# First loads through another queue and a re-planned order: attention and channel mix on one core

## The chip, the cores and the metric

The kernel runs on one core of a Trainium2 chip. A core has TensorE (matrix products, into the accumulation memory PSUM), VectorE, ScalarE and GpSimd (elementwise work), and SyncE, which issues DMAs; GpSimd issues DMAs too. Each engine runs its own instructions in a fixed order, and waits on semaphores for the others. The metric is the device time of one execution in microseconds. Seven runs of the kernel before took 241.66 to 243.84 us, with a median of 242.81.

## The reference

Two stages, with 8 batches, 8 heads, 576 positions, head size 64, in fp32:

```python
rel = pos[:, None] - pos[None, :]
mask = (rel >= 0) & (rel < 128)
scores = where(mask, q @ k.T / sqrt(64) - slopes[h] * abs(rel), -1e9)
x = (softmax(scores) @ v) with heads side by side      # [8, 576, 512]

x_prev = x shifted by one position
xk = mu_k * x + (1 - mu_k) * x_prev
xr = mu_r * x + (1 - mu_r) * x_prev
kk = relu(xk @ w_k) ** 2                               # 512 -> 1024
out = sigmoid(xr @ w_r) * (kk @ w_v)                   # 1024 -> 512
```

## The kernel before

All products run in bf16. A batch is worked in four groups of two heads. A window of 128 positions over tiles of 128 means that a key tile meets only its own query tile and the next one, so scores are computed key by query in strips (line 548), exponentiated by ScalarE (line 559), and multiplied with v on TensorE (line 603); a column of ones beside v gives the row sums, whose reciprocal (line 609) scales the result (line 614). The bias comes in one of two ways. For the first `NBIAS` groups TensorE adds it before the exponential (line 535, from the distances `dist` and a scaled identity `sid`); later VectorE multiplies the exponentials with a table (line 572). The result is turned by TensorE (line 641), copied by ScalarE to `xt` (line 518, as all of `copy_any`), and VectorE makes the difference to the shifted copy (line 667) and the two mixtures `xk` and `xr` (line 674).

The channel mix takes stretches of 256, 384 or 512 positions: eight times four products with w_k (line 754), a relu on ScalarE (761), a square on VectorE or ScalarE (727, 725; `SQ` says who may), then for each tile of 128 positions four products with w_r (772), a tanh on ScalarE (779), eight products with w_v (786), and one VectorE operation that joins both (797) and is stored by SyncE (803).

Queries and keys must lie with the head dimension on the partitions. Batches 1 to 3 are loaded and turned by TensorE (line 918, then a ScalarE copy of 128x1024). Batches from 4 on (`XB`) are turned by DMA transposes that SyncE issues (`flip`, line 397). Batch 0 is worked in two parts, positions 0 to 255 and the rest, so that work can start early: its part 0 of groups 0 and 1 comes in fp32 through SyncE (`first_load`, line 409) into `stage`, is cast to bf16 on ScalarE or VectorE and turned on TensorE (line 850). Part 0 of groups 2 and 3, and part 1 of all, come through GpSimd's queue, whose DMAs cast on their way (`half_load`, line 368).

All other loads stand in GpSimd's queue, in the order of the string `LOADS`: `v` and `V` the first and second half of v of batch 0, `0` and `1` queries and keys of part 0 for groups 2 and 3, `K` and `k` the halves of w_k, `2` and `3` queries and keys of part 1, `t` the last 64 positions, `a`, `b`, `c` batch 1, `R` w_r, `W` and `w` the halves of w_v. The batches 2 to 7 follow.

The order of the instructions on the engines is not written by hand. The kernel adds each piece of work to a `Plan` with an estimated duration, what it depends on, and a priority; `Plan.run` fills the engines in estimated time, and the order that comes out is what the program holds. `A`, `SLOPE`, `NBIAS`, the estimates in `dma` and `flip`, and the lists of engines that may do a thing are inputs to this plan: change one and many instructions move. `NWARM` = 90 products on a tile of zeros (line 509) keep TensorE running at the beginning, with the lowest priority.

Constant columns, those of ones beside v, the pads of `at`, `xt`, `tt` and the unused half of `tv`, are set by VectorE memsets in the opening (line 336).

Of the kernel before, what the change touches and what calls it, by code (L numbers as in the profile page):

```python
# [150 lines left out]
def kernel(  # L151
# [27 lines left out]
    RELU_SCALE = 0.5 ** 0.5  # L179

    NQ, NA, NX, NV, NC = 4, 4, 3, 2, 2
    XB = range(4, B)
    XO = range(6, B)
    X0 = 16
    NWARM = 90
    LOADS = 'v01Kk23tVabcRWw'
    XD = 4
    OTL = 5.0
    NO = 4

# [3 lines left out]
    def SQ(order):  # L194
        return (DVE, ACT) if order < 10 else (DVE,)

    def XT(b, g):
        return (ACT,)

# [3 lines left out]
    def many(n, shape, dtype, name):  # L203
# [10 lines left out]
        "p (a i r h d) -> p a i r h d", a=2, i=2, r=2, d=D)  # L214
    stage = qx_buf[1].rearrange("p i g s -> p (i g s)").bitcast(FP32)[:, 0:8 * 2 * D].rearrange(
        "p (i g h w) -> p i g h w", i=2, g=2, h=2)
    at_buf = many(NA, [128, 2 * 1024 + 64], BF16, "at")
# [29 lines left out]
    def one(h):  # L247
        return uno[h.idx if h.cls == "p1" else N1 + h.idx]

    def two(h):  # L250
# [4 lines left out]
                {})  # L255
    PE, ACT, DVE, POOL, SPE, FAB, VIR = "PE", "ACT", "DVE", "POOL", "SP", "FAB", "VIR"
    LAT = {PE: 0.2, ACT: 0.22, DVE: 0.16}

    def mm(n):
        return max(n / 2400.0 + 0.0025, 0.029)  # L260
# [7 lines left out]
    AHEAD = 30.0  # L268
    A = {PE: 9.00, ACT: 7.00, DVE: 5.50, VIR: 0}
    NBIAS = 4  # L270
    XRL = 3.0
    MODE = 0
    EARLY = 0.0
    SLOPE = 4.8

# [22 lines left out]

    def dma(queue, kb, issue, emit, deps=(), need=(), free=(), after=()):
        n = plan.add(queue, issue, 0.0, list(deps) + [last.get(queue)],  # L300
                     (len(plan.nodes),), emit, need)
        last[queue] = n
        return plan.add(FAB, kb / 290.0, 0.9, [(n, 1.0)], (len(plan.nodes),),
                        None, (), free)
# [30 lines left out]
    def memset(t, v, dur=0.08, late=0):  # L335
        return dve_op(dur, lambda e: nc.vector.memset(t, v), [], (0, 20 + late))
# [6 lines left out]
    n_ident = dve_op(0.11, emit_ident, [n_iota], (0, -1))  # L343
    blank, blank_t, blank_v = [], [], []
    for t in range(NA):
        blank.append(memset(at_buf[t][:, 2048:2112], 1.0))
        blank.append(memset(at_buf[t][:, 1024:1088], 1.0))
    for t in range(NV):
        blank_v.append(memset(vs_buf[t][:, :, :, D], 1.0, 0.08, -21))
    for t in range(2):  # L350
        blank.append(memset(xt_buf[t][:, :, X0 - 2:X0], 0.0))
        blank.append(memset(tt_buf[t][:, :, 1], 0.0))
    for t in range(NV):
        blank_t.append(memset(tv_buf[t][64:128], 0.0, 0.5, 1))
        blank_t.append(memset(tv_buf[t][0:64, :, D], 1.0, 0.08, 1))

    def issue_t(nd):
# [36 lines left out]
    def flip(b, i, j, g):  # L396
        return dma(SPE, 290, 1.3, lambda e: nc.sync.dma_start_transpose(
            out=qx_buf[xbh[b].idx][:, i, :, 128 * j:128 * j + 128],
            in_=cb_buf[ch[b].idx][:, i, j].rearrange("p h d -> p (h d)")),
            [g, (cl[b][NF * i + j], 6.0)], (), [ch[b]])  # L400
# [4 lines left out]

    def first_load(i, g):
        hs = (q, k)[i][0, 2 * g:2 * g + 2]
        dst = stage[:, i, g]
        return dma(SPE, 128, 0.46, lambda e: nc.sync.dma_start(
            out=dst, in_=hs[:, 0:256].rearrange("h (p r) d -> p h (r d)", p=128)))  # L410

    def mu_load(i, src):
        return dma(SPE, 4, 0.5, lambda e: nc.sync.dma_start(
            out=mu_row[NPO * i:NPO * i + NPO], in_=src.rearrange("(po p) -> po p", p=128)))
# [4 lines left out]
    src0 = {}  # L419
    for g in range(2):  # L420
        for i in range(2):
            src0[i, g] = [first_load(i, g)]
    n_row = [mu_load(0, moe_mu_k), mu_load(1, moe_mu_r)]
# [3 lines left out]
    def load_step(what):  # L427
        if what in "01":
            for r in range(2):
                rs_ = half_load(int(what), 0, r, 4, 8)  # L430
                for g in (2, 3):
                    src0.setdefault((int(what), g), []).append(rs_)
        elif what in "vV":
            for j in ((0, 1) if what == "v" else (2, 3)):
                vl[0].append(v_load(0, j, vh[0], [gv[0]] + blank_v))
                if j == 0:
                    n_w["d"] = pool_op(0.55, emit_cut, [n_ident, last[POOL]])
                    last[POOL] = n_w["d"]
            if what == "V":
                vl[0].append(tv_load(0, vh[0]))  # L440
        elif what in "23":
            src1.extend(half_load(int(what) - 2, 1, r, 0, 8) for r in range(2))
        elif what == "t":
            th[0], tl[0] = tail_load(0)
        elif what in "Kk":
            j = int(what == "k")
            n_w["k", j] = w_load(wk_sb[:, :, 512 * j:512 * j + 512],
                                 moe_w_k[:, 512 * j:512 * j + 512], 780)
        elif what == "R":
            n_w["r"] = w_load(wr_sb, moe_w_r, 840)  # L450
        elif what in "Ww":
            j = int(what == "w")
            n_w["v", j] = w_load(wv_sb[:, 4 * j:4 * j + 4], moe_w_v[512 * j:512 * j + 512], 790)
        elif what in "abc":
            batch_load(1, what)
# [41 lines left out]
    def emit_mu(e):  # L497
# [3 lines left out]
        out=id_row, in_=ident[0:2 * NPO, 0:2 * NPO]), [n_ident], (0, 3))  # L501
    n_mut = plan.add(PE, 0.1, LAT[PE], n_row + [n_idr], (0, 0), emit_mu, [h_mu])
    n_muk = n_mur = plan.add(DVE, 0.08, LAT[DVE], [n_mut], (0, 4), lambda e: nc.vector.tensor_copy(
# [8 lines left out]
    for i in range(NWARM):  # L512
        plan.add(PE, 0.1 if i < 40 else 0.056, 0.0, [n_warm, g_wm], (1e12, i), emit_warm, (), [h_wm])

# [224 lines left out]
    def channel_mix(P, c0, c1, first, xks, xrs, order):  # L739
# [27 lines left out]
        for i, c in enumerate(range(c0 // 128, c1 // 128)):  # L767
# [13 lines left out]
            hv, ho = Hold("p1"), Hold("ot")  # L781
            o = 128 * c - c0

            def emit2(e, half, hv=hv, o=o):
                for fo in range(4 * half, 4 * half + 4):
                    nc.tensor.matmul(  # L786
                        one(hv), lhsT=kk_buf[hk.idx][:, fo, o:o + 128], rhs=wv_sb[:, fo],
                        start=(fo == 0), stop=(fo == NFO - 1))
            m0 = op(PE, NPO * mm(512), squares[0:4] + [n_wv[0]], place(),
                    lambda e, f=emit2: f(e, 0), [hv], [hk])  # L790
            m1 = op(PE, NPO * mm(512), squares[4:8] + [n_wv[1], m0], place(),
                    lambda e, f=emit2: f(e, 1), (), [hk])

            pe_mix.extend((m0, m1))

            def emit_o(e, hv=hv, hs=hs, ho=ho):
                nc.vector.scalar_tensor_tensor(  # L797
                    out=ot_buf[ho.idx], in0=rs_buf[hs.idx], scalar=1.0, in1=one(hv),
                    op0=ALU.add, op1=ALU.mult)
            d = op(DVE, dve_t(512), [m1, t], place(), emit_o, [ho], [hv, hs])  # L800
            row = SP * P + 128 * c
            y = plan.add(SPE, 0.6, 0.0, [d], (1, len(plan.nodes)),
                         lambda e, ho=ho, row=row: nc.sync.dma_start(
                out=of[row:row + 128, :], in_=ot_buf[ho.idx]))
            plan.add(FAB, 0.8, 0.9, [(y, 1.0)], (0,))
            plan.add(VIR, 0.0001, 0.0, [(y, OTL)], (0,), None, (), [ho])

# [22 lines left out]
    for part in range(2):  # L830
        if part == 1:
            htt, n_tt = tails(0, (0, 0, 1, 0))
        for g in range(G):
            prio = (0, 0, part, g)
            if part == 0 and g < 2:
                cs = []
                for i in range(2):
                    cs.append(op((ACT, DVE), {ACT: act_t(256, True), DVE: dve_t(256, 2)},
                                 src0[i, g], prio + (0,), lambda e, i=i, g=g: copy_any(
                        e, half_buf[:, 0, i, :, 2 * g:2 * g + 2].rearrange("p r h d -> p h r d"),  # L840
                        stage[:, i, g].rearrange("p h (r d) -> p h r d", d=D))))
            else:
                cs = src0[0, g] + src0[1, g] if part == 0 else src1
            hp = Hold("p1")

            def emit_t(e, part=part, g=g, hp=hp):
                for i in range(2):
# [7 lines left out]
                   [hp] + ([hq0[g]] if part == 0 else []))  # L855
            y = op((ACT, DVE), {ACT: act_t(512), DVE: dve_t(512)}, [t], prio + (3,),
                   lambda e, part=part, g=g, hp=hp: copy_any(
# [6 lines left out]
            for j, (pieces, m0) in enumerate(PART[part]):  # L864
# [7 lines left out]
            t0, t1 = ((0, 2), (2, NJ))[part]  # L872
            r, hx = attend(0, g, t0, t1, ha, es + vl[0][0:2] + (vl[0][2:] + blank_t if part else []) + blank,
                           prio)
# [107 lines left out]
```

## Time and profile before

| | us |
|---|---|
| median of 7 runs | 242.81 |
| profiled execution, whole | 241.43 |
| its span, first to last instruction | 239.7 |
| TensorE busy | 226.1 (94%), 2183 products |
| VectorE busy | 185.6 (77%) |
| ScalarE busy | 164.4 (69%) |
| GpSimd busy | 105.1 (44%) |
| first product of the channel mix (L754) | starts at 16.48 |
| first product with w_r (L772) | starts at 40.00 |
| last product (L786) | ends at 235.7 |

The profile takes one execution apart. Busy time alone says little of what a change is worth; the chain that ended last is followed back from the last instruction, at each step to what released it, and shows which engine or DMA set the end in which part of the span. A group in the profile is named by its line, engine, what it writes and what it reads, with buffer numbers left out. Products on TensorE overlap, so that one listed with 379 ns starts 0.215 us after the one before it. The clock that TensorE was granted is 1.00 nearly everywhere, with 0.50 for 3.41 us after 16.19.

### The profile page before, as it was taken

The page shows a single profiled execution, that of the slowest core. Times are in us where ns is not written, and L with a number is a line of the kernel's source. Part 1 is how long each engine was busy: PE and PEld are TensorE (multiplying, and loading weights), DVE is VectorE, ACT ScalarE, POOL GpSimd, SP SyncE. Part 2 cuts the span into 40 slices and gives each one's busy share as a digit, 9 for nine tenths or more (in the row PEclk, how much of TensorE's full clock was granted, in tenths as well). Part 3 has the DMA queues.
Part 4 walks back from the last instruction along what each step waited for, and adds up shares of the span by engine and source line. Part 5 has one row for each costly group of instructions (what it writes and reads, how often), then busy time and mean ns, then how long its engine had stood idle before and what let it go on. Part 6 is the DMA issues. An engine that isn't in the chain of part 4 may idle for free.

```text
span 239.7 us, 5684 instructions
## 1 busy us (share of the span) xinstructions
PE 226.1 (94%) x2183; PEld 139.1 (58%) x2211; DVE 185.6 (77%) x407; ACT 164.4 (69%) x289; POOL 105.1 (44%) x132
## 2 busy tenths in 40 slices
PE   8979977999999999799999999999999999999993
PEld 8647564666666765355655666455655754445561
DVE  7575596799998989579897989985789975894342
ACT  3468989779997986778496895957482925326260
POOL 8958995598998961069405953300000000000000
PEclk9988999999999999999999999999999999999998
DMA  8999999999999999999998999996331214221212
GB/s 122 129 178 139 147 130 186 169 180 190 195 139 172 169 165 130 204 164 159 165 195 74 158 163 158 200 134 155 90 100 54 80 54 91 88 88 46 88 45 88
DMA packets 141755, 32.23 MB, mean 134 GB/s; under 512 B 133528, under 2 KB 137120, under 8 KB 141728
## 3 DMA queue, kind: packets, MB, share of 16 engines
q0 software_dynamic: 113104, 16.52, 112.0%
q1 hardware_dynamic: 28624, 15.35, 31.7%
q8 instruction: 17, 0.28, 0.5%
q14 instruction: 10, 0.08, 0.1%
HBM read 33.56 MB, written 9.44 MB: 179 GB/s over the span
## 4 chain that ended last, share of the span: by engine, by line
PE 75%; DMA 14%; POOL 5%; ACT 2%; issue 2%; DVE 1%; POOLq 0%; DVEq 0%
PE uno L786 25%; PE uno L754 22%; PE uno L772 12%; PE duo L603 6%; PE duo L548 5%; DMA wk_sb<-in_moe_w_k_dram 4%; DMA qx<-cb 4%; DMA wr_sb<-in_moe_w_r_dram 3%; DMA vs<-in_v_dram 3%; PE uno L641 2%; POOL vs L371 2%; POOL qx L368 1%; PE uno L918 1%; ACT at L559 1%; POOL cb L393 1%
## 5 line engine op out<-in xcount | busy, mean ns | idle before, releaser
L754 PE MATMUL uno<-xk,wk_sb 128*128 128x256 bf16 (+2 forms) x413 | 71.7, 318 | 1.5 <-ACT xt L518 0.7
L559 ACT ACTIVATE at<-duo 128x1024 bf16<-128x1024 f32 (+2 forms) x68 | 65.1, 1001 | 10.3 <-PE duo L548 10.2
L786 PE MATMUL uno<-wv_sb,kk 128*128 128x512 bf16 x274 | 69.8, 379 | 0.8 <-issue 0.2
L761 ACT ACTIVATE rl<-uno 128x256 bf16<-128x256 f32 (+2 forms) x104 | 47.0, 493 | 22.9 <-PE uno L754 22.3
L754 PEld LDWEIGHTS <-wk_sb 128*128 128x128 bf16 x416 | 39.5, 99 | 25.0 <-issue 2.6
L371 POOL DMA_DIRECT2D vs<-in_v_dram x32 | 28.4, 903 | 30.8 <-PE duo L603 27.0
L786 PEld LDWEIGHTS <-kk 128*128 128x128 bf16 x288 | 26.1, 98 | 26.1
L572 DVE TENSOR_TENSOR at<-at,mask 128x1024 bf16<-128x1024 bf16 x56 | 37.2, 681 | 4.9 <-ACT at L559 4.7
L727 DVE TENSOR_TENSOR kk<-rl 128x256 bf16<-128x256 bf16 (+2 forms) x77 | 25.6, 342 | 17.9 <-ACT rl L761 16.5
L779 ACT ACTIVATE rs<-uno 128x512 bf16<-128x512 f32 x36 | 22.2, 617 | 24.9 <-PE uno L772 24.8
L772 PE MATMUL uno<-wr_sb,xr 128*128 128x512 bf16 x133 | 35.9, 379 | 2.0 <-DMA wr_sb<-in_moe_w_r_dram 1.5
L797 DVE SCALAR_TENSOR_TENSOR ot<-rs,uno 128x512 f32<-128x512 bf16 x36 | 24.5, 683 | 13.6 <-PE uno L786 8.5
L393 POOL DMA_DIRECT2D cb<-in_k_dram x28 | 24.8, 893 | 9.2 <-DMA wv_sb<-in_moe_w_v_dram 3.3
L674 DVE SCALAR_TENSOR_TENSOR xk<-dl,mu_sb,xt 128x576 bf16<-128x576 bf16 (+2 forms) x36 | 26.4, 746 | 0.5
L674 DVE SCALAR_TENSOR_TENSOR xr<-dl,mu_sb,xt 128x576 bf16<-128x576 bf16 (+2 forms) x36 | 26.3, 740 | 0.0
L393 POOL DMA_DIRECT2D cb<-in_q_dram x28 | 24.9, 910 | 2.2 <-DMA vs<-in_v_dram 0.7
L603 PEld LDWEIGHTS <-at 128*128 128x128 bf16 x576 | 21.9, 98 | 5.8 <-ACT at L559 0.3
L772 PEld LDWEIGHTS <-xr 128*128 128x128 bf16 x144 | 13.5, 98 | 15.7 <-DMA wr_sb<-in_moe_w_r_dram 1.7
L518 ACT COPY xt<-uno 128x576 bf16<-128x576 bf16 (+2 forms) x28 | 15.9, 578 | 7.6 <-PE uno L641 7.6
L603 PE MATMUL duo<-vs,at 128*128 128x65 bf16 x448 | 19.1, 194 | 0.1
L614 DVE TENSOR_TENSOR xu<-duo,rc 128x640 bf16<-128x640 f32 x20 | 16.4, 820 | 0.5
L667 DVE TENSOR_TENSOR dl<-xt 128x576 bf16<-128x576 bf16 (+2 forms) x36 | 14.7, 421 | 2.3 <-ACT xt L518 2.0
(64 smaller groups left out, 219.1 us busy)
## 6 DMA issues: line engine op xcount, KB each, us to landing
out_dram<-ot SPq DMA_DIRECT2D x36, 256.0 KB, 3.6
vs<-in_v_dram POOLq DMA_DIRECT2D x32, 128.0 KB, 6.5
cb<-in_q_dram POOLq DMA_DIRECT2D x28, 128.0 KB, 7.5
cb<-in_k_dram POOLq DMA_DIRECT2D x28, 128.0 KB, 8.9
wk_sb<-in_moe_w_k_dram POOLq DMA_DIRECT2D x2, 512.0 KB, 7.6
wv_sb<-in_moe_w_v_dram POOLq DMA_DIRECT2D x2, 512.0 KB, 10.8
ts<-in_q_dram POOLq DMA_DIRECT2D x8, 64.0 KB, 7.7
ts<-in_k_dram POOLq DMA_DIRECT2D x8, 64.0 KB, 7.6
```

The lines of the kernel that those rows point to most:

```text
L371: return dma(POOL, 256, issue_t(1024), lambda e: nc.gpsimd.dma_start(out=vs_buf[h.idx][:, j, :, 0:D], in_=v[b, :, 128 * j:128 * j + 128].r ...
L393: return [dma(POOL, 256, issue_t(1024), lambda e, r=r: nc.gpsimd.dma_start(out=cb_buf[h.idx][:, i, r], in_=src[:, :, r]), [g]) for r in ra ...
L559: lambda e, ah=ah, w=w, hp=hp: nc.scalar.activation(out=ah(), in_=two(hp)[:, :, 0:w], func=AF.Exp, scale=float(scale)), (), [hp])
L572: nc.vector.tensor_tensor(out=a, in0=a, in1=m, op=ALU.mult)
L603: nc.tensor.matmul(a[:, hl, t - t0], lhsT=at[:, lo:lo + 128], rhs=vs[:, u, 2 * g + hl, :] if u < NF else tvb[:, 2 * g + hl], start=(u == u ...
L674: lambda e: nc.vector.scalar_tensor_tensor(out=buf[hk.idx][:, g, e0 + c0:e0 + c1], in0=dls(), scalar=mu[:, g:g + 1], in1=xc(1), op0=ALU.mu ...
L727: nc.vector.tensor_tensor(out=out, in0=in_, in1=in_, op=ALU.mult)
L754: nc.tensor.matmul(one(hp)[:, 0:n], lhsT=wk_sb[:, po, 128 * fo:128 * fo + 128], rhs=xk_buf[hx.idx][:, po, c0:c1], start=(po == 0), stop=(p ...
L761: a = op(ACT, act_t(n), [s], pr, lambda e, hp=hp, hr=hr: nc.scalar.activation(out=rl_buf[hr.idx][:, 0:n], in_=one(hp)[:, 0:n], func=AF.Rel ...
L772: nc.tensor.matmul(one(hp), lhsT=xr_buf[hx.idx][:, po, 128 * c:128 * c + 128], rhs=wr_sb[:, po], start=(po == 0), stop=(po == NPO - 1))
L786: nc.tensor.matmul(one(hv), lhsT=kk_buf[hk.idx][:, fo, o:o + 128], rhs=wv_sb[:, fo], start=(fo == 0), stop=(fo == NFO - 1))
L797: nc.vector.scalar_tensor_tensor(out=ot_buf[ho.idx], in0=rs_buf[hs.idx], scalar=1.0, in1=one(hv), op0=ALU.add, op1=ALU.mult)
```

## The change

Batch 0's part 0 now comes whole through SyncE: after the four loads of groups 0 and 1 two larger ones bring groups 2 and 3, into a `stage` of twice the size. All eight casts are ScalarE's, the copies after the transposes may be ScalarE's or VectorE's. The loads `0` and `1` leave GpSimd's queue; `K` moves up behind the first half of v, and `k` moves back behind the second half of v. The memsets of the pads are split: those of v's column of ones, of the middle pads of `at` and of `xt` stay at the front, the others (`blanks`) are put behind the fourth SyncE load in the plan. The last tile of the output is computed in two column pieces, 384 and 128 wide, each with its own products, join and store. Batch 4 leaves `XB`, so TensorE turns it as it does batches 1 to 3. ScalarE may take squares in the first 3 stretches of the channel mix, and no more in the first 10. `NBIAS` goes from 4 to 5, and the plan's inputs `A`, `SLOPE`, the DMA rate and latency, the estimate of a flip and of a few short operations are changed.

The diff, cut to its core:

```diff
-    XB = range(4, B)
+    XB = range(5, B)
-    LOADS = 'v01Kk23tVabcRWw'
+    LOADS = 'vK23tVkabcRWw'
+    FIN = 384
+    RATE = 284.0
+    FLIP = 1.25
     def SQ(order):
-        return (DVE, ACT) if order < 10 else (DVE,)
+        return (DVE, ACT) if order < 3 else (DVE,)
+    XT0 = (ACT,)
+    QK0 = (ACT, DVE)
+    CAST = (ACT,)
-    stage = qx_buf[1].rearrange("p i g s -> p (i g s)").bitcast(FP32)[:, 0:8 * 2 * D].rearrange(
-        "p (i g h w) -> p i g h w", i=2, g=2, h=2)
+    stage = qx_buf[1].rearrange("p i g s -> p (i g s)").bitcast(FP32).rearrange(
+        "p (i g h w) -> p i g h w", i=2, g=4, h=2)
-    A = {PE: 9.00, ACT: 7.00, DVE: 5.50, VIR: 0}
-    NBIAS = 4
+    A = {PE: 8.75, ACT: 4.50, DVE: 6.75, VIR: 0}
+    NBIAS = 5
-    SLOPE = 4.8
+    SLOPE = 4.7
-        return plan.add(FAB, kb / 290.0, 0.9, [(n, 1.0)], (len(plan.nodes),),
+        return plan.add(FAB, kb / RATE, lat[1], [(n, lat[0])], (len(plan.nodes),),
                         None, (), free)
...
+    blank_v = [memset(vs_buf[t][:, :, :, D], 1.0, 0.09, -21) for t in range(NV)]
     for t in range(NA):
-        blank.append(memset(at_buf[t][:, 2048:2112], 1.0))
-        blank.append(memset(at_buf[t][:, 1024:1088], 1.0))
+        memset(at_buf[t][:, 1024:1088], 1.0)
     for t in range(2):
-        blank.append(memset(xt_buf[t][:, :, X0 - 2:X0], 0.0))
-        blank.append(memset(tt_buf[t][:, :, 1], 0.0))
-    for t in range(NV):
-        blank_t.append(memset(tv_buf[t][64:128], 0.0, 0.5, 1))
-        blank_t.append(memset(tv_buf[t][0:64, :, D], 1.0, 0.08, 1))
+        memset(xt_buf[t][:, :, X0 - 2:X0], 0.0)
+    def blanks(after):
...
+        for t in range(2):
+            late(tv_buf[t][64:128], 0.0, 0.55)
+            late(tv_buf[t][0:64, :, D], 1.0)
+        for t in range(2):
+            late(tt_buf[t][:, :, 1], 0.0, 0.17)
+        for t in range(NA):
+            late(at_buf[t][:, 2048:2112], 1.0)
...
-    def first_load(i, g):
-        hs = (q, k)[i][0, 2 * g:2 * g + 2]
-        dst = stage[:, i, g]
+    def first_load(i, g, n):
+        hs = (q, k)[i][0, 2 * g:2 * g + 2 * n]
+        dst = stage[:, i, g:g + n].rearrange("p g h w -> p (g h) w")
...
-    for g in range(2):
+    for g, n in ((0, 1), (1, 1), (2, 2)):
         for i in range(2):
-            src0[i, g] = [first_load(i, g)]
+            x = first_load(i, g, n)
+            for j in range(g, g + n):
+                src0[i, j] = [x]
+    blank = blanks(src0[1, 1][0])
     def load_step(what):
-        if what in "01":
-            for r in range(2):
-                rs_ = half_load(int(what), 0, r, 4, 8)
-                for g in (2, 3):
-                    src0.setdefault((int(what), g), []).append(rs_)
...
-                vl[0].append(tv_load(0, vh[0]))
+                vl[0].append(tv_load(0, vh[0], blank[0:4]))
...
+            final = row + 128 == B * S
...
+            for a, b in ((0, FIN), (FIN, 512)) if final else ((0, 512),):
+                for half in range(2):
+                    first = a == 0 and half == 0
+                    m = op(PE, NPO * mm(b - a), squares[4 * half:4 * half + 4] +
+                           [n_wv[half], m], place(),
+                           lambda e, f=emit2, h=half, a=a, b=b: f(e, 4 * h, 4 * h + 4, a, b),
+                           [hv] if first else [], [hk])
+                    pe_mix.append(m)
+                d = op(DVE, dve_t(b - a), [m, t], place(),
+                       lambda e, f=emit_o, a=a, b=b: f(e, a, b), [ho] if a == 0 else [], [hv, hs])
...
-            if part == 0 and g < 2:
+            if part == 0:
...
-                    cs.append(op((ACT, DVE), {ACT: act_t(256, True), DVE: dve_t(256, 2)},
+                    cs.append(op(CAST, {ACT: act_t(256, True), DVE: dve_t(256, 2) + 0.08},
...
-            y = op((ACT, DVE), {ACT: act_t(512), DVE: dve_t(512)}, [t], prio + (3,),
+            y = op(QK0, {ACT: act_t(512), DVE: dve_t(512)}, [t], prio + (3,),
...
-            r, hx = attend(0, g, t0, t1, ha, es + vl[0][0:2] + (vl[0][2:] + blank_t if part else []) + blank,
+            r, hx = attend(0, g, t0, t1, ha, es + vl[0][0:2] + (vl[0][2:] + blank if part else []),
                            prio)
```

## The prediction, made before the result was known

> **What bounds the kernel now.** I read the chain that ended last, whole and then in order of time, next TensorE's waits, then busy time by stage. Engine shares of the chain first:
>
> ```profile
> PE 75%; DMA 14%; POOL 5%; ACT 2%; issue 2%; DVE 1%; POOLq 0%; DVEq 0%
> ```
>
> The same chain over the first 45 us (start us, us, what):
>
> ```profile
> 3.81 3.02 POOL qx L368 x4
> 6.83 0.72 POOL wk_sb L403
> 7.54 8.51 DMA wk_sb<-in_moe_w_k_dram
> ...
> 31.79 8.16 DMA wr_sb<-in_moe_w_r_dram
> 39.95 0.05 issue
> 40.00 0.39 PE uno L772
> ```
>
> Until 40 us the chain is GpSimd's load queue; from then on it is TensorE without a break but one. The first is four loads of query and key heads standing in the queue ahead of the weights. The waits of TensorE say how much is lost after the opening:
>
> ```profile
> PE uno L772 <- DMA wr_sb<-in_moe_w_r_dram: 1.5, 1, 1.5
> PE duo L548 <- DMA qx<-cb: 1.3, 1, 1.3
> ```
>
> The second is batch 4 waiting for its last transposing DMA at 97.8. Busy time by stage (stage and length, TensorE, its weight loads, VectorE, ScalarE, GpSimd; clock, DMA share, GB/s):
>
> ```profile
> 0.00:16.48 16.48, 13.39 (x164) 10.64 (x165) 10.79 (x53) 7.15 (x13) 13.37 (x23) 0.99 1.26 142
> 16.48:40.00 23.52, 20.10 (x249) 14.06 (x248) 16.52 (x46) 21.05 (x45) 20.62 (x25) 0.93 2.35 146
> 40.00:97.00 57.00, 56.38 (x639) 37.16 (x648) 52.13 (x100) 49.31 (x82) 41.73 (x50) 1.00 2.21 169
> 97.00:100.00 3.00, 1.67 (x16) 0.69 (x16) 2.02 (x4) 2.36 (x5) 0.00 (x0) 1.00 1.73 203
> 100.00:235.76 135.76, 134.55 (x1120) 76.55 (x1136) 103.51 (x206) 84.56 (x147) 29.33 (x35) 1.00 1.02 116
> ```
>
> TensorE is 99% busy from 40 on, so the span splits in three: the moment T at which the first multiplication by w_r starts (39.95), TensorE's work behind it (235.68 - 39.95 = 195.7, of which 1.5 is the gap at 97.8), and the tail (239.7 - 235.7 = 4.0):
>
> ```profile
> 233.08 2.60 PE uno L786 x12
> 235.68 0.04 DVEq L797
> 235.72 0.04 issue
> 235.76 0.69 DVE ot L797
> ```
>
> One store follows: 3.25 us from the end of that VectorE row to the end of the span. The change touches all three parts.
>
> **Work behind T.** The listing of instructions shows what moves.
> - Batch 4 takes its queries and keys by 32 TensorE transposes instead of eight transposing DMAs. The chain shows eight such transposes of L918 in 0.45 us: +1.8 us. Four copies of 128x1024 come to ScalarE (1057 ns each in the L518 row, +4.2 us); in 40-97 it is busy 49.3 of 57, and it gives squares away, so I put them at nothing. Without that cover they would cost at most 4.2.
> - The gap of 1.5 us at 97.8 goes. Late next would be batch 5's transposing DMAs. Before, they were issued behind batch 4's and landed by 107, while in the new order 80 us of TensorE's work stand between T and the first product that needs them, which puts it near 118. Eight issues of 1.2 to 2.2 us leave SyncE's queue; what stands beside batch 5's eight is one output store behind the first. So no new gap: -1.5.
> - Eight w_k multiplications (256 wide; 28 take 3.06 us in the chain, 0.11 each) move ahead of T: -0.87 here, paid in the opening.
> - 17 of ScalarE's 27 squares (rows of L725) become VectorE's. By the rows of L727 VectorE gains 9 x 0.288 + 3 x 0.355 + 5 x 0.420 = 5.8 us, and loses two mask products of 0.681, because batch 1's first group takes its bias on TensorE. VectorE is 91% busy in 40-97. In the listing, counting row durations, VectorE's work from batch 1's first to batch 6's first reciprocal goes from 143 - 29 = 114 to 144 - 27 = 117 us, and TensorE's for the same stretch from 115 to 113. That is tight, but VectorE overlaps neighbours, so its own time is less than the sum. Between 0 and 4.4 us; I take 0, since the VectorE work listed ahead of batch 1's first reciprocal falls from 29.4 to 27.1 us, a head start of 2.3.
> Sum: 195.7 - 1.5 + 1.8 - 0.9 = **195.1**.
>
> **Tail.** The last tile's eight w_v products become eight of 384 columns, then eight of 128. Columns and so TensorE's time stay the same. VectorE's last operation shrinks from 0.69 (512) to near the 0.42 of the 256-wide product of L614, or less: -0.3 to -0.4. The last store carries 64 KB instead of 256; the transfer's gain I bound between 0 (the first piece's 192 KB go ahead of it, and SyncE issued stores in 0.33 to 0.54 us each) and -0.9 (192 KB less at the 203 GB/s of the row 97-100). I take -0.15, near the first bound, as both pieces must pass one queue within half a us. In all -0.5: **3.5**.
>
> **The opening, T.** Two conditions, the later one counts.
>
> *w_r landed.* Removed from GpSimd's queue: the 3.02 us of issue above. w_k's first half, which landed at 13.5 (6.81 + 6.7), is then issued near 3.8. The second half goes behind the second-half queries and keys, two tails and the rest of v. The bytes do not vanish: two SyncE loads of 256 KB share the DMA engines. Here a rule speaks against the change. The Trainium skill (DMA: Bandwidth & Descriptors, "Issuing engines are not separate DMA queues") says that DMAs from SyncE and GpSimd interleave on the same 16 engines, so a second issuer saves only issue time; and its "Rules for kernel authors" give a load that casts to GpSimd. By the rule w_r gains 1 us (3.0 less about 2 for the moved bytes). By the row more: DMA moved 116 GB/s in 0-9.4 and 178 in 9.4-16.3, so it was short of issued work in the first stretch, and in the second the first w_k half was late although nothing else was queued. I take 2.5, between 1.0 and 3.0: landing at 37.5.
>
> *TensorE reaches it.* ScalarE paces 16-40: 21.05 of 23.52, against 7.15 of 16.48 earlier. All eight fp32 casts (405 ns; two were ScalarE's) now stand in its order, five before the first exponential and three before the second, so that one waits for the last SyncE load. SyncE's small loads landed 2.4 to 3.6 us after issue; the last two are issued near 2.8 and 3.3, carry twice the bytes and share the engines, so I take 7.5 and 8.8. First exponential then at 7.5 (before 7.48), second at 10 (9.48), third 12.2 (12.60), fourth 13.6 (13.3), the last copy of part 0 at 16.3 (16.05). The casts use time in which ScalarE sat idle (3.18 us before 7.48); without that cover they cost 6 x 0.405 = 2.4. The gain comes after: second-half queries and keys, landed at 20 before, are there before 16, so part 1's transposes start at about 15.9 instead of 20.27. From 16.3 on, ScalarE's listed work until batch 1's copies, counted from each start to the next since neighbours overlap, is 3 copies (0.50), 8 masks (0.33), 4 + 4 exponentials (0.70, 0.50), 8 relus (0.30), 3 squares (0.32) and 4 copies (0.35): 13.7 us, ready at 30.0 against 31.36. Batch 1's loads, which landed at 31.0, come 2.5 earlier too. Then 7.1 us as before to TensorE's idle at 38.5, plus what moved ahead: 0.87 and four bias products (0.215 each in L772's row of the chain), 0.86, of which some 0.7 falls into the 1.6 us of small gaps there: 30.0 + 7.1 + 1.0 = **38.1**.
>
> So T = 38.1, set by ScalarE and TensorE and no more by w_r. w_r's stall is gone, ScalarE is late next.
>
> A second rule is weighed. The granted clock was 0.50 from 16.19 to 19.60:
>
> ```profile
> 16.19:19.60 3.41, 3.08 (x14) 0.50 2.42 156
> ```
>
> That row cost 1.7 us of TensorE. The Trainium skill (TensorE: Matmul & The Clock Gate, "Part 4: PE-mode transpose") says that transposes do not count as activity, and Part 1 that full speed needs a busy window of about 3.4 us. TensorE now resumes with 20 transposes where 20 matmuls stood: by the rule the half clock lasts a window longer, +1.7. By the row the part is paced by ScalarE, so neither is worth much; I take 0, and keep both ends, -1.7 and +1.7.
>
> **Sum.** 38.1 + 195.1 + 3.5 = 236.7 against 239.7: -3.0. The profiled execution took 241.43, so 238.4; the median of the runs shown is 1.4 above it (242.81). Measured times are medians, so I forecast 242.81 - 3.0 = **239.8**, own range 238.4 to 241.3.
>
> **Rivals.**
> 1. *The queue delivers at once.* w_r at 37.0, half clock gone, ScalarE gains the 1.7: T near 36.6. 36.6 + 195.1 + 3.5 = 235.2, so 238.3. For it: queue issue led the chain. Against: ScalarE 90% busy in 16-40.
> 2. *The opening gains nothing.* The last SyncE loads turn with v and w_k packet by packet and land as late as GpSimd's did (10.5; TensorE waited for them until 10.59). Both later exponentials shift by 2 us and T is 40.3; what is left is -1.5 + 1.8 - 0.9 - 0.5, some -0.8: 242.0. This is also the case that the change doesn't do what it says.
> 3. *VectorE becomes the bound* (slower). Place: 40 to 150, where it takes the squares. Price: the 4.4 us above, if none of its idle 4.9 us in 40-97 can be used, because each idle piece is a wait for ScalarE; TensorE then waits for VectorE's products before the next multiplication. 236.7 + 4.4 = 241.1, so 244.3. It decides once over two thirds of the added work goes uncovered. For it: 91%; against: the head start.
>
> **Chances.** Forecast 0.52, rival 1 0.18, rival 2 0.16, rival 3 0.14. No change means within 0.5%, 241.6 to 244.0, about what the runs' spread of 241.66 to 243.84 lets one tell. Faster: nearly all of the forecast, rival 1 and a quarter of rival 2, 0.71; same 0.16; slower 0.13. The range runs from rival 1 less the half clock's rest, 237.6, to the far side of rival 2, 243.2.
>
> **What will show it.** Right: first w_r multiplication near 38 without a DMA wait; part 1's transposes before 17; no wait of L559 for a transposing DMA; ScalarE over 90% busy from 16 to 38; end of span less than 3.6 after TensorE's last product. Wrong: w_k's second half or v late and TensorE waiting for it near 22; a second exponential after 11; VectorE named in TensorE's waits between 40 and 150; a half clock beyond 20.

## The result, and the profile after

| | before | after |
|---|---|---|
| median, us (runs, lowest to highest) | 242.56 (31, 241.09 to 244.86) | 238.99 (12, 238.33 to 240.65) |
| ratio, 95% interval | | 0.9852, 0.9825 to 0.988 |
| profiled execution / its span, us | 241.43 / 239.7 | 239.1 / 237.3 |
| first w_r product starts (T) | 40.00 | 38.41 |
| from T to the end of the last product | 195.67 | 196.05 |
| from there to the end of the span | 4.0 | 2.8 |

The kernel is 3.57 us faster: 238.99, where 239.8 was forecast with a range of 237.6 to 243.2. The profiled spans differ by less, 2.4 us, for the profile of the kernel before was taken in one of its quicker executions: 241.43, 1.1 under the median, where that of the kernel after (239.1) lies at its median.

In the page after, the chain that ended last has these shares by engine:

```profile
PE 84%; ACT 6%; DMA 4%; POOL 2%; issue 2%; DVE 0%; POOLq 0%; DVEq 0%; ACTq 0%
```

DMA had 14% of it. The chain over the first 45 us in order of time (start us, us, what) shows what is gone:

```profile
4.60 2.59 POOL qx L381 x3
7.19 9.53 DMA qx<-in_k_dram
17.04 1.08 ACT qk L529 x2
...
30.41 1.05 PE uno L935 x16
...
34.94 2.00 ACT at L570 x2
...
38.84 0.59 PE uno L783 x2
```

The load of w_r, 8.16 us of this chain before, is no longer in it; T is reached through ScalarE's exponentials and relus and TensorE. What is left of the DMAs is the second half of the keys, which landed at 16.72 (20.0 before). Busy time by stage (stage and length, TensorE, its weight loads, VectorE, ScalarE, GpSimd; clock, DMA share, GB/s):

```profile
0.00:15.60 15.60, 12.33 (x164) 9.62 (x165) 10.31 (x49) 8.70 (x17) 12.34 (x21) 1.00 1.48 167
15.60:38.41 22.81, 20.31 (x262) 14.48 (x262) 15.62 (x45) 21.10 (x47) 19.99 (x24) 1.00 2.07 160
38.41:97.00 58.59, 57.69 (x653) 37.83 (x661) 52.83 (x103) 50.88 (x81) 40.86 (x50) 1.00 2.10 169
97.00:100.00 3.00, 3.00 (x35) 1.77 (x34) 3.00 (x8) 3.00 (x6) 0.00 (x0) 1.00 1.09 111
```

Three things are to be seen. ScalarE is busy 21.10 of the 22.81 us ahead of T, 93%: it sets the pace there. TensorE is busy for the whole of 97 to 100, where it stood 1.3 us before, for batch 4 needs no transposing DMA now. And the granted clock is 1.00 in every row shown, with no 3.41 us at half speed.

TensorE's waits (line, what it waited for: us in total, times, longest) hold no DMA wait for w_r or for `qx<-cb`, but behind T a new one:

```profile
PE uno L799 <- DVE ot L804: 0.7, 1, 0.7
```

It lies in the tail, as the end of the chain shows:

```profile
230.99 2.18 PE uno L799 x12
...
233.24 0.56 DVE ot L804
233.81 0.04 issue
233.85 0.62 PE uno L799 x8
234.47 0.02 issue
234.50 0.29 DVE ot L804
```

The products of the second column piece start only when VectorE has read the first: the start of the second group comes 0.87 us later than the usual distance between products. The diff suggests why: both pieces use one `hv`, so one PSUM buffer, and the read of one part of it holds up the writes to the other. An experiment below tests it.

### The profile page after: what moved, and what is told of

It reads as the page before. It is cut to its first block, busy times and chain, and to the rows that moved or that the text cites. A ratio compares the mean times of both kernels' runs of the same rounds, so it can differ in the third digit from the quotient of the medians.

```text
span 237.3 us, 5756 instructions
## 1 busy us (share of the span) xinstructions
PE 225.9 (95%) x2225; PEld 140.0 (59%) x2255; DVE 186.8 (79%) x420; ACT 164.9 (69%) x283; POOL 102.6 (43%) x128
## 4 chain that ended last, share of the span: by engine, by line
PE 84%; ACT 6%; DMA 4%; POOL 2%; issue 2%; DVE 0%; POOLq 0%; DVEq 0%; ACTq 0%
PE uno L799 26%; PE uno L765 25%; PE uno L783 13%; PE duo L614 7%; PE duo L559 6%; DMA qx<-in_k_dram 4%; PE uno L935 3%; PE uno L652 2%; ACT qk L529 2%; ACT at L570 1%; ACT rl L772 1%; POOL qx L381 1%; ACT xt L529 1%; PE uno L716 1%; ACT mask L900 1%
## 5 line engine op out<-in xcount | busy, mean ns | idle before, releaser
L799 PE MATMUL uno<-wv_sb,kk 128*128 128x512 bf16 (+2 forms) x282 | 69.8, 373 | 1.7 <-DVE ot L804 0.7
L765 PE MATMUL uno<-xk,wk_sb 128*128 128x256 bf16 (+2 forms) x412 | 69.2, 313 | 0.4 <-ACT rl L772 0.2
L772 ACT ACTIVATE rl<-uno 128x256 bf16<-128x256 f32 (+2 forms) x104 | 47.9, 486 | 16.5 <-PE uno L765 14.8
L765 PEld LDWEIGHTS <-wk_sb 128*128 128x128 bf16 x416 | 38.9, 98 | 21.7 <-issue 0.2
L738 DVE TENSOR_TENSOR kk<-rl 128x256 bf16<-128x256 bf16 (+2 forms) x94 | 30.4, 338 | 15.5 <-ACT rl L772 14.4
L799 PEld LDWEIGHTS <-kk 128*128 128x128 bf16 x296 | 26.6, 98 | 26.4 <-issue 0.9
L583 DVE TENSOR_TENSOR at<-at,mask 128x1024 bf16<-128x1024 bf16 x54 | 36.1, 677 | 4.0 <-ACT at L570 4.0
L783 PE MATMUL uno<-wr_sb,xr 128*128 128x512 bf16 x133 | 36.4, 379 | 0.6
L804 DVE SCALAR_TENSOR_TENSOR ot<-rs,uno 128x512 f32<-128x512 bf16 (+2 forms) x37 | 24.6, 666 | 14.1 <-PE uno L799 10.5
L529 ACT COPY qk<-uno 128x1024 bf16<-128x1024 bf16 (+1 forms) x20 | 18.1, 943 | 4.3 <-PE uno L935 2.7
```

What stands on the lines that cost most here:

```text
L529: (nc.scalar.copy if e == ACT else nc.vector.tensor_copy)(out=out, in_=in_)
L583: nc.vector.tensor_tensor(out=a, in0=a, in1=m, op=ALU.mult)
L738: nc.vector.tensor_tensor(out=out, in0=in_, in1=in_, op=ALU.mult)
L765: nc.tensor.matmul(one(hp)[:, 0:n], lhsT=wk_sb[:, po, 128 * fo:128 * fo + 128], rhs=xk_buf[hx.idx][:, po, c0:c1], start=(po == 0), stop=(p ...
L772: a = op(ACT, act_t(n), [s], pr, lambda e, hp=hp, hr=hr: nc.scalar.activation(out=rl_buf[hr.idx][:, 0:n], in_=one(hp)[:, 0:n], func=AF.Rel ...
L783: nc.tensor.matmul(one(hp), lhsT=xr_buf[hx.idx][:, po, 128 * c:128 * c + 128], rhs=wr_sb[:, po], start=(po == 0), stop=(po == NPO - 1))
```

## The experiments

Kernels that start from the one after are "after with ..."; the others start from the one before. T and the work behind it are from each one's profiled execution. The kernel before was run again beside each set of experiments, with medians of 241.94, 242.52 and 241.69 us, where it had 242.56 beside the kernel after; so differences under about 1 us between two sets are not told apart.

### The tail: one piece, or a buffer for each piece

After, with the last tile in one piece as before:

```diff
-            final = row + 128 == B * S
+            final = False
```

> The kernel after with the last tile in one piece again; nothing else moves. In the profile after, the last store begins its way 1.2 us sooner behind the last product than before, but TensorE waits 0.87 us for VectorE between the two pieces. Theory 1 (the split is worth its two terms, -1.2 and +0.9): 0.3 us slower than the kernel after, so about 0.987 of the kernel before. Rival (the split is worth what the prediction said, 0.5): 0.5 us slower. Third (worth nothing): same as after within 0.2. Profile: span behind the last product 4.0 us, no wait of L799 for L804.

Measured: 238.86 us (238.53 to 241.05), ratio to before 0.9883, 0.9842 to 0.9924; T 38.03, then 195.17, then 3.8. The new wait is gone, and the time is that of the kernel after (238.99). So the split as it was made is worth nothing that can be measured: what it gains in VectorE and in the store (together 1.0 us) it gives back in the wait (0.87).

After, with a PSUM buffer of its own for the second piece:

```diff
+                if a:
+                    hv = Hold("p1")
...
```

> The kernel after with the second piece of the last tile in a PSUM buffer of its own. Theory 1 (TensorE's wait between the pieces comes from both pieces lying in one buffer, which VectorE still reads): the wait of 0.87 us goes, the first store keeps its distance to the second, and the time falls by 0.5 to 0.9 us below the kernel after, to about 0.982 of the kernel before. Rival (the last store is held by the first one or by SyncE, not by TensorE): the wait goes and the end stays, within 0.2 us of the kernel after.

Measured: 238.43 us (237.85 to 240.51), ratio 0.9877, 0.9831 to 0.9923, with four of six runs at 237.85 to 238.81. In its profile the wait is gone. From T to the last product it takes 195.18 us, as with one piece, so the wait was the shared buffer's. The span is 236.3 against 237.3, but 0.65 of that lies in an earlier T (37.76). From T to the end of the span it takes 198.5, where the kernel after takes 198.9 and the one with a single piece 199.0: the buffer is worth 0.4 us, less than the 0.5 to 0.9 expected, and in the medians that is not clear of the noise.

With `FIN = 256` besides, so two pieces of 256 columns:

> The kernel after with the last tile in two halves of 256 columns, each in a PSUM buffer of its own. Theory 1 (the last store's way starts when VectorE has done the second piece; its length does not depend on the bytes): VectorE's last operation (about 0.42) starts at the last product's end, so the end is as in the run with 384 and 128 columns in two buffers, within 0.3 us, about 0.985 of before. Rival (a smaller last store lands sooner): 0.3 us or more slower than that run.

Measured: 237.82 us (237.39 to 238.54), ratio 0.9849, 0.9811 to 0.9887, the lowest median of all, 1.2 us under the kernel after and with intervals that overlap its own. From T to the end of the span it is 198.5 again, as expected. VectorE's two joins take 0.42 us each. How far the bytes of a store count can be read off here: from the issue of the last store to the end of the span it took 3.2 and 3.0 us with 256 KB (before, and the tail in one piece), 2.7 with 128 KB here, and 2.5 and 2.7 with 64 KB (after, and the two buffers above).

### The loads: the queue of before in the kernel after

After, with groups 2 and 3 of part 0 by GpSimd's queue again:

```diff
-    LOADS = 'vK23tVkabcRWw'
+    LOADS = 'v01Kk23tVabcRWw'
...
-    for g, n in ((0, 1), (1, 1), (2, 2)):
+    for g, n in ((0, 1), (1, 1)):
...
```

> The kernel after with the loads of before: groups 2 and 3 of part 0 by GpSimd's queue, w_k as before; memsets, casts on ScalarE, plan inputs, batch 4 and tail as after. Theory 1 (the loads are what brings the first product with w_r forward, by 1.5 us, and they keep the clock up): that product at 40 or later with a wait for w_r's DMA, half clock in the opening again, 1.5 to 2.5 us slower than after. Rival (memsets and the plan's inputs bring it): less than 0.7 us slower.

Measured: 242.21 us (241.09 to 243.5, 12 runs), ratio 1.0014, 0.9987 to 1.0042. T is 40.37, and 197.73 follow, with one stretch of 3.41 us at half clock. Without the loads the whole of the gain is gone, 2.0 us of it at T and 1.7 behind it (half of the latter, 0.87, is eight products with w_k that stand ahead of T in the kernel after, 60 against 52, and behind it here and before). So the loads are necessary. But the wait for w_r that was expected did not come: w_r landed at 40.20, late again by 3.0 us, yet just ahead of T. What held T is in the chain:

```profile
10.85 9.78 DMA qx<-in_k_dram
20.67 0.47 PE uno L872 x5
...
34.50 1.94 ACT qk L534 x2
```

The second half of the keys landed at 20.63 (16.72 after), so batch 1's copies began on ScalarE at 33.59 (31.05 after). The old queue delays two things by 3 to 4 us, w_r and these keys, and either is late enough to hold T. Whether the new loads are enough is the next question.

### The opening alone, and batch 4 alone

Before, with the opening's loads and casts, and nothing else:

```diff
-    LOADS = 'v01Kk23tVabcRWw'
+    LOADS = 'vK23tVkabcRWw'
...
-    def first_load(i, g):
+    def first_load(i, g, n):
...
-            if part == 0 and g < 2:
+            if part == 0:
...
-                    cs.append(op((ACT, DVE), {ACT: act_t(256, True), DVE: dve_t(256, 2)},
+                    cs.append(op((ACT,), {ACT: act_t(256, True), DVE: dve_t(256, 2)},
```

> The kernel before with the opening's loads and casts alone: part 0 whole through SyncE, w_k's halves and v in the new order, casts on ScalarE; memsets at the front, batch 4 by DMA, squares, plan inputs and tail as before. Theory 1 (the loads bring the first product with w_r forward, to about 38.4 us, and end the half clock; putting the old loads back into the kernel after cost about 3 us): 2 to 3 us faster than the kernel before, w_r no more waited for. Rival (new loads help only together with the new plan inputs): within 0.7 us of before. Third (the transposing DMAs of batches 4 to 7 then come late, as in the run with batch 4 back on DMAs): slower than before, with waits of L548 for qx<-cb of 2 us or more.

Measured: 249.87 us (249.59 to 253.02), ratio 1.0311, 1.0249 to 1.0372. T falls to 37.80, so the opening does what it should, but 206.16 us follow. TensorE's longest wait here:

```profile
PE duo L550 <- DVE tt L520: 2.9, 1, 2.9
```

and the chain through it:

```profile
58.43 0.46 DVE dl L669
58.88 0.73 DVE xr L676
59.61 0.06 DVE xk L676
59.67 0.58 issue
60.26 0.45 DVE dl L669
60.71 0.21 DVE tt L520
...
61.21 5.21 PE uno L756 x16
```

VectorE is busy throughout 55 to 59.4 (the row below); the copy `tt`, 0.21 us long and next in TensorE's need, stands in VectorE's fixed order behind differences and mixtures (`dl`, `xk`, `xr`). And then comes the price that a wait alone doesn't have (windows of the same kernel):

```profile
55.00:59.40 4.40, 2.33 (x34) 1.71 (x31) 4.40 (x8) 4.26 (x6) 3.60 (x6) 1.00 2.23 190
59.40:66.23 6.83, 5.26 (x18) 2.35 (x18) 5.50 (x10) 2.97 (x6) 6.42 (x8) 0.50 2.15 162
```

TensorE stood from 58.09 to 60.97. The half clock (0.50) began within that wait and lasted 6.83 us. A second wait, of 2.0 us for VectorE's `ot` before 123.37, was followed by another 3.41 us of it. By an estimate from these numbers, half of TensorE's busy time at half clock being lost (2.6 and 1.7), the two waits and what followed make 9.2 of the 10.5 us that the work behind T grew by.

Before, with batch 4 turned by TensorE, and nothing else:

```diff
-    XB = range(4, B)
+    XB = range(5, B)
```

> The kernel before with batch 4 turned on TensorE and nothing else changed. Theory 1 (+1.8 us of TensorE work against the gap of 1.5 us): within 0.7 us of the kernel before. Rival (batch 4's DMAs delay more than their own gap, as the 14 us lost with them in the kernel after suggests): 1.5 us or more faster than before.

Measured: 242.77 us (241.28 to 244.13, 12 runs) beside 242.52, ratio 0.9992, 0.9958 to 1.0027. The wait for `qx<-cb` is gone from its profile and the transposes are in it; within the interval, about 0.9 us either way, the two pay for each other, as +1.8 and -1.5 said.

Before, with both:

> The kernel before with the opening's loads and casts and with batch 4 turned on TensorE, together; each alone gave no gain (1.031 and 0.999 of before). Theory 2 (the opening pays only if the order behind it has no late transposing DMAs and no overfull VectorE; batch 4 on TensorE takes the DMAs away): the first product with w_r near 38, no wait over 1 us behind it, 1 to 2.5 us faster than before. Rival (what the kernel after needs are the plan's inputs and squares, which were fitted to its opening): within 1 us of before or slower, with a wait for VectorE of 2 us or more behind 45, as in the run with the opening alone.

Measured: 248.33 us (246.92 to 249.9), ratio 1.0279, 1.0231 to 1.0326. T is 38.20, and the wait for `tt` is there again with 2.9 us and again 6.83 us at half clock with it. So loads, casts and batch 4 together are not enough: the rest of the change is what lets the kernel keep the gain. It is made of the plan's inputs, the squares, the memsets, the tail and a few estimates.

### Which part of the rest

After, with the plan's inputs of before:

```diff
-    RATE = 284.0
-    FLIP = 1.25
+    RATE = 290.0
+    FLIP = 1.0
-    A = {PE: 8.75, ACT: 4.50, DVE: 6.75, VIR: 0}
-    NBIAS = 5
+    A = {PE: 9.00, ACT: 7.00, DVE: 5.50, VIR: 0}
+    NBIAS = 4
-    SLOPE = 4.7
+    SLOPE = 4.8
```

> The kernel after with the plan's inputs of before (A, NBIAS, SLOPE, DMA rate, flip). Loads, casts, batch 4, squares and tail as after. Theory 1 (the gain is in loads and batch 4, the inputs are worth little): within 0.7 us of the kernel after; 0.86 us of TensorE work for batch 1's bias is saved. Rival (the inputs decide): 1.5 us or more slower, with TensorE waiting in the opening for ScalarE or for w_r.

Measured: 240.94 us (240.12 to 241.42), ratio 0.9906, 0.9869 to 0.9942. That is 2.0 us above the kernel after by the medians and 1.3 by the ratios, with intervals that just overlap. T is 39.58 though w_r landed at 36.51: between 28 and T TensorE waits five times for ScalarE, 0.5 to 0.6 us each, and there is one stretch at half clock in the opening.

After, with ScalarE's share of the squares of before:

```diff
-        return (DVE, ACT) if order < 3 else (DVE,)
+        return (DVE, ACT) if order < 10 else (DVE,)
```

> The kernel after with ScalarE allowed to take squares in the first 10 stretches again. Theory 1 (VectorE covers the squares: TensorE has no wait for VectorE in 40 to 150 in the kernel after): within 0.5 us of the kernel after. Rival (moving the squares off ScalarE is what lets ScalarE keep up with batch 4's copies): 1 us or more slower, waits of TensorE for ScalarE in 80 to 110.

Measured: 240.65 us (240.07 to 241.23), ratio 0.9892, 0.985 to 0.9935, so 1.7 us above the kernel after by the medians and 1.0 by the ratios, with intervals that overlap; the profiled span is 1.2 longer. T is 37.70, and 197.95 follow. The added time lies in five small gaps ahead of products with w_k, 0.45, 0.50, 0.28, 0.21 and 0.37 us between 135 and 214. The first is ScalarE's:

```profile
135.25 0.20 ACT kk L736
...
135.55 0.43 ACT rl L772
...
136.02 0.60 PE uno L765 x4
```

A square (`kk`) stands ahead of the relu (`rl`) that empties PSUM for TensorE. For the others the waits name `xk` and `ot` of VectorE, and a relu.

After, with the memsets at the front again (`res.append(memset(t, v, dur))` in `blanks`):

> The kernel after with all memsets in front of VectorE's copies again. Theory 1 (VectorE has room in the first 6 us): within 0.4 us of the kernel after. Rival (the memsets delay the first copies of queries and keys, as the row before with 0.62 and 0.49 us before the first copy suggests): first exponential later than 7.5 by 0.3 us or more, and 0.5 to 1 us slower than after.

Measured: 238.70 us (237.88 to 239.9), ratio 0.9888, 0.9844 to 0.9931; T 38.18. They ran from 3.4 to 5.9 us instead of 5.5 to 8.1, and the first exponential started at 6.55, no later than after (7.53). No difference shows in the time. But w_r landed at 38.14 in this profile, and TensorE waited 0.7 us for it.

None of the three brings the wait for `tt` back. Each of the first two costs 1 to 2 us, and what keeps VectorE's order clear at 58 us, one of them, both, or one of the estimates left untested, stays open.

### Batch 4 on the DMAs in the kernel after

```diff
-    XB = range(5, B)
+    XB = range(4, B)
```

> The kernel after with batch 4 turned by transposing DMAs again. Theory 1 (the gap before L559 at 97.8 us came from these DMAs, 1.5 us, and the 32 TensorE transposes cost 1.8): TensorE's work falls by 1.8 us and a gap of 1 to 2 us before L559 waiting for qx<-cb comes back near batch 4; time within 0.5 us of the kernel after. Rival (the transposing DMAs also slow other loads, so taking them away was worth more): 1 us or more slower than after. Other rival (the gap was chance, batch 4's DMAs now come in time): 1.5 us faster than after.

Measured: 252.87 us (247.4 to 255.26). Five of the six runs took 252.1 or more, with mean clocks of 0.966 to 0.973, and one took 247.4 with 0.986; even that one is 8.4 us above the kernel after. The profile is of one of the five. No gap of 1.5 us came back at batch 4. The costliest wait of TensorE:

```profile
PE duo L559 <- DMA qx<-cb: 5.4, 3, 2.8
```

SyncE's own queue in order of time (start, us, what) tells what happened:

```profile
115.23 1.60 SPq L410 DMA_TRANSPOSE qx<-cb  x1
116.93 11.53 SPq L820 DMA_DIRECT2D out_dram<-ot  x2
128.60 1.71 SPq L410 DMA_TRANSPOSE qx<-cb  x1
```

SyncE takes its instructions in order. Two output stores took 11.53 us of the queue, 9.6 of them the second one's wait for VectorE, which had made its tile only at 128.1. The transposing DMAs behind it, which had nothing to do with that tile, were issued that much later; those of batch 6 landed up to 151.9, after TensorE had reached them. Two stretches of 6.83 us at half clock followed, the second with another 5.2 us of waits, for VectorE's `xk` near 221; what delayed that is not followed up here. In this order, then, batch 4's place on TensorE is worth far more than the 1.5 us of its own gap, at least 8.4: eight issues leave a queue that the stores share. In the order of the kernel before it was worth nothing, so this is a matter of the order too.

### The clock

After, with half of the products on zeros:

```diff
-    NWARM = 90
+    NWARM = 45
```

> The kernel after with 45 products on zeros instead of 90, so that none stands behind the 11th us. Theory 1 (these products keep the clock full through the resumption at 15.6, transposes or not): half clock for 3.4 us somewhere between 14 and 24, and 0.5 to 1.7 us slower than after. Rival (the kernel's own products are activity enough): clock full as in the kernel after, within 0.4 us. By the rule that transposes do not count, the half clock would last 6.8 us and cost up to 3.4.

Measured: 241.27 us (238.66 to 242.3, 12 runs), ratio 0.9974, 0.9936 to 1.0011. Its mean clock was 0.983 to 0.986 in seven runs (240.52 to 242.3), 0.992 or 0.993 in four (239.91 to 240.91) and 1.00 in one, which took 238.66, the time of the kernel after. In the profiled run, with a mean clock of 0.993, one window of 3.4 us is at half speed:

```profile
18.00:21.40 3.40, 3.40 (x21) 1.31 (x19) 2.07 (x6) 2.51 (x4) 2.69 (x4) 0.50 1.78 177
21.40:25.00 3.60, 3.60 (x52) 2.22 (x51) 0.88 (x3) 3.22 (x8) 3.07 (x5) 0.99 2.42 155
```

A window of 3.41 us at half clock takes 0.007 off the mean of such a span (half clock after the last product, which costs nothing, took off up to 0.003 more in the profiles), so the seven runs had about two windows, one more than the profile shows. The products on zeros, then, keep the clock of the kernel after, and their loss costs about 2 us. In the profiles, 41 of the 90 start after 10 us in the kernel after, and 17 in the kernel before: they move into the gaps of the opening without a line of the diff about them.

The same shows, less sharply, in the kernel before. Of its 53 runs beside the experiments, seven had a mean clock of 0.996 or more, with a median of 241.49 us (240.15 to 243.23); 34 had 0.989 to 0.993, about one window, as in its profile (0.990), with 241.81; 12 had 0.982 to 0.986, about two, with 243.55. The kernel after had 0.996 to 1.00 in eleven of twelve runs (238.33 to 239.43, median 238.97), and 0.993 in the slowest (240.65). At nearly full clock the two kernels stand 2.5 us apart, about what the spans show. Of the other 1.1 of the 3.57, runs of the kernel before with two windows are a part; how large a part is not shown, for one window costs little in the median, the times at one clock spread over 3 us, and the clocks of the 31 runs behind 242.56 are not known.

## Why the prediction was right, and where its terms were off

**T.** Forecast 38.1, measured 38.41, and 37.76 to 38.32 in the four versions that differ in tail or memsets only. The named cause is the one seen: w_r landed at 37.24 (37.5 forecast) and isn't waited for, and ScalarE, 93% busy, is late next. The two are close: w_r landed between 36.66 and 38.14 in those four, and in the one with the memsets at the front it set T. Its steps: the last SyncE loads landed at 7.19 and 8.20 (7.5 and 8.8); the exponentials started at 7.53, 9.18, 11.92 and 13.16 (7.5, 10, 12.2, 13.6); the last copy of part 0 at 15.79 (16.3); batch 1's copies at 31.05 (30.0). The last is the step that was a microsecond off: the transposes of part 1 did start at 15.59, but most of them waited until the keys landed at 16.72. The stretch from there to T took 7.4 us where 8.1 was reckoned, so that two errors nearly cancel.

**The rule on issuing engines.** The Trainium skill (DMA: Bandwidth & Descriptors, "Issuing engines are not separate DMA queues") says that a second issuer saves issue time only. The issue time taken off GpSimd's queue was 3.02 us and w_r came 2.7 earlier, so the trace agrees with that sentence. What failed is the 2 us taken off for the moved bytes, by which the forecast read 1 us out of the rule: the engines had room for them. In 0 to 9.4 us they moved 116 GB/s before and 119 with the old loads put back, but 169 after. The first rival, a queue that delivers at once with w_r at 37.0, was nearly right on the landing and yet wrong on T, because ScalarE holds it; its own T of 36.6 lies ahead of its landing, which cannot be.

**Work behind T.** Forecast 195.1, measured 195.17 to 195.32 in the three kernels without the tail's wait. Batch 4 alone fits +1.8 against -1.5, and the eight products with w_k did move ahead of T (60 against 52). But "no new gap" was argued from batch 5's due time, and the danger was elsewhere: with batch 4 on the DMAs SyncE's queue holds up batch 6. That eight issues leave the queue was given as a reason and priced at nothing; in the new order it is worth at least 8.4 us.

**The squares.** They were put at 0, between 0 and 4.4 as a cost. They are no cost: back on ScalarE, in a plan made anew around them, the kernel is not faster but 1.0 to 1.7 us slower, though not clear of the noise. The lower bound of nothing was perhaps too high. Only one of the five gaps there (0.45 us) is shown to come from a square ahead of a relu; what made the others stays open. The third rival, VectorE as the bound in 40 to 150, did not come in the kernel after (52.83 of 58.59 busy ahead of 97, and no wait of TensorE for VectorE up to 150). In the opening alone TensorE did wait for VectorE, and it cost more than the 4.4 priced, but not by the rival's mechanism: the squares were still where they had been, and one short copy stood too late in VectorE's order. The rival's 244.3 should be 244.2 (242.81 + 241.1 - 239.7).

**Tail.** Forecast 3.5, measured 2.8 plus a wait of 0.87, in all 3.7. Two errors nearly cancel, which is luck. The store gained more than the 0.15 taken: 3.2 us from its issue to the end became 2.5. And TensorE's time was said to stay the same, which overlooked the wait for a shared PSUM buffer, the step of the sum whose mechanism was wrong.

**Half clock.** Put at 0 between -1.7 and +1.7. By what the Trainium skill says of transposes (TensorE: Matmul & The Clock Gate, "Part 4: PE-mode transpose"), that they do not count as TensorE being busy in the same way, it would have lasted a window longer. No run here decides that. The row 15.60:38.41 has 1.00 throughout although TensorE resumed with transposes, but products on zeros kept TensorE busy until just ahead of them, at 15 us; and with 45 of these the profile has one window where most of the runs had about two, at places that no profile shows. In the profile's sum the term is nearly nothing, as taken: at 0.996 or above the kernel before has a median of 241.49, and its profiled execution, with one window, took 241.43.

**The sum and the medians.** That 239.8 came within 0.8 of 238.99 is in part luck. For the profiled spans the sum of -3.0 was 0.6 too much (the tail's wait and 0.3 at T, less the store). In the other direction, the 1.4 us by which the kernel before ran above its profiled execution was carried over to the kernel after, whose median lies 0.1 under its own. So the steadier clock of the kernel after was worth more than the 0 that it was put at, by an amount that stays open.

## What to carry to other kernels

A stage that a planner orders can't be changed one edit at a time: the same opening gave -1.5% with the order re-made around it and +3.1% without, in large part because one short copy in an in-order engine came late. When an edit takes work off a queue, ask what stands behind that queue's slowest wait, since what leaves may be worth more to its neighbours than its own stall. And when a last tile is split, give each piece an accumulation buffer of its own, else the read of one piece holds back the products of the next: it took the whole gain of the split here.

## What the runs showed of the hardware

- In the profiles half clock comes, up to the last product, in stretches of 3.41 us or twice that, and it differs between executions of one program. Waits of 2.9 us of TensorE went with 6.83 us of it in two kernels, and one of 2.0 us with 3.41; one of 2.1 us, for w_r in the kernel with batch 4 alone, had none behind it. So the length of a wait alone does not say what it costs.
- The time from a last store's issue to the end of the span changes little with its bytes: 3.0 and 3.2 us for 256 KB, 2.7 for 128, 2.5 and 2.7 for 64.
- A store that waited 9.6 us for VectorE held up the transposing DMAs behind it in the same queue, and the kernel, with the waits and the half clock that came with it, took 8.4 to 16.3 us more than the kernel after.
